# A fused forward and backward kernel: load order and transposes at the start, the gate as row sums, and the last tile in halves

## The chip, the cores and the metric

The kernel runs as one program on one core of one Trainium2 chip. A core has five engines that run at the same time, each through its own instructions in order: TensorE (PE in the profile) multiplies matrices and transposes tiles into PSUM; VectorE (DVE) and ScalarE (ACT) do elementwise work and read PSUM out; GpSimd (POOL) and SyncE (SP) here mostly issue DMAs. Engines wait for each other by semaphores. The metric is the device time of one execution in microseconds (us); lower is better. Three executions of the kernel before took 1215.14, 1215.94 and 1216.46 us, median 1215.94.

## What is computed

A gated mix of two branches, and its gradients for a given `grad_out`:

```python
x = A_x                                               # 1 x 2048 x 1024, bfloat16
g = sigmoid((x * gate_w).sum(-1, keepdims=True))      # one number per row
a = irfft2(rfft2(x) * (w_r + 1j * w_i))               # spectral filter over 2048 x 1024
h = x @ w1 + b1                                       # 1024 -> 3584
b = relu(h) ** 2 @ w2 + b2                            # 3584 -> 1024
out = g * a + (1 - g) * b
# and jax.vjp: the gradients of x, w_r, w_i, w1, b1, w2, b2 and gate_w
```

There are nine outputs: `out` and eight gradients.

## The kernel before

Rows are handled in 16 tiles of 128; the 3584 hidden columns (F) in 28 chunks of 128 (`fc`), 1024 (D) in 8 chunks (`dc`). PE's work is laid out in three main stages: `mlp_in` (hidden products and their gradients), `mlp_grads` (gradients of w1 and w2) and `mlp_out` (the output and the gradient of x). The spectral branch is a side generator (`aside`, L1721), cut into several hundred steps; `spread` (L1607) mixes its steps into the main stages at rates worked out from the number of steps left (`first_rate`, `rate`, `last_rate`; the total is the formula of L1747). The order in which the program emits instructions is the order on each engine, except where a dependency ("paced", `after`, L234) holds one back; a `NoSync` dependency fixes an order on one engine without a wait. DMAs are issued by SP (`ld`), POOL (`st`) or ACT.

**The start.** `mlp_in` first does `fc` 0 to 3 (two w1 pairs `fp` 0 and 1, each of two chunks) for four blocks of 512 rows (`s`), one unit per `next(units)`: for every `s` four hidden units (`forth`, L757) and then four gradient units (`back_`, L763). A hidden unit is 8 products 128x512 `ph` (L725), then on ACT a ReLU `rT` (L726) and a square `h2T` (L727). A gradient unit is 8 products `pd` (L733) and on DVE one scalar_tensor_tensor (L737) with `rT`. The products need x and the gradient transposed: `turn_tile` (L636) makes 8 PE transposes of a row tile into PSUM tile `pt` (two buffers, shared with the gate) and one copy into `xT` (ACT, or DVE for tiles 1 and 3) or `dbT` (DVE). Before a gradient tile is turned it is scaled by 1 - g: `gate` (L649) makes the row sums of x*gate_w for four tiles with 32 PE products one column wide (`pg`, L655) against `gwcol` (the gate row as a column, turned by `vectors`, L643), two sigmoids on ACT (`omg`, `gcol`) and four scalings of `dbn` on DVE (L662).

The loop at L1666 weaves this for each `s`: turning of grad tiles and x tiles, the gate and, behind unit 7, steps of the spectral first stage (11 of them in the start). SP's loads are x0 to x3, w1 pair 0, grad 0 to 3, w1 pair 1, two transposing loads of w2 (L181), x4 to x7, grad 4 to 7, and then the spectral stage's sources (`src`) mixed with the other x and grad tiles. POOL loads the constants `kf`, `flip`, `sel` and `cf` early. x tiles for turning have four buffers (`xsrc`).

**The middle.** In `folded` (L546) of the spectral output stage ACT copies the even parts (`re`, L553) and DVE makes folds `rf` (L558, L559); both are input of PE's products `pki` (L566). The copies are held, by `turn["ACT"]`, behind the newest ordered ACT instruction of the main stage, whatever that is: a copy that frees a PSUM bank, or a scaling in `prepare` (L1254) or `close` (L1264).

**The last stage.** `mlp_out` is made of Strassen-like blocks (`Block`, L1320 on): seven chains of 14 products (`chain`, L1337) on quarter matrices, `p1` to `p7`, into PSUM banks `X` and `V`; ACT copies `X` out (`kept`, L1347: `c1`, `u2`, `u3`), DVE adds a bank and a kept copy into `cu` (L1360). "h" blocks make `out`, "d" blocks the gradient of x. `right` (L1398) makes the differences of right operands `T1` to `T4` on DVE. In the last "h" block (k == NB-1), `right(T1, ...)` (L1503) stands ahead of `put` (L1276) and `prepare` of the next tiles. The last "d" block ends with p5, p7, p4 and p3; between p4 and p3 the gate gradient's row is made (L1590 to L1593). The block's tile 14 is finished by `close_x` (L1309) after p3: DVE adds p3's bank and u2 into cu's right half, adds v over the whole width and SP stores 128x1024.

Of the kernel before, what the change touches and what calls it, by code (L numbers as in the profile page):

```python
# [10 lines left out]
P = 128  # L11
# [129 lines left out]
def kernel(  # L141
# [67 lines left out]
    gwcol = cols("gwcol", [DC], BF16)  # L209
# [31 lines left out]
    turn = {"PE": None, "DVE": None, "ACT": None}  # L241
# [288 lines left out]
    def fft_out():  # L530
# [15 lines left out]
        def folded(n):  # L546
# [5 lines left out]
            for im in range(2):  # L552
# [3 lines left out]
                ), "ACT")  # L556
# [73 lines left out]

    def source(i, view, earlier=None, tag="src"):
        src = f1.tile([P, D], BF16, name=tag, tag=tag, bufs=4)
        after(ld(out=src[:], in_=view[i]), earlier)
        return src

    def turn_tile(dst, i, src, copy):  # L636

        pt = tps.tile([P, DC, P], BF16, name="pt", tag="tr", bufs=2)
        for b in range(DC):
            nc.tensor.transpose(pt[:, b, :], src[:, b * P : (b + 1) * P], identb[:])  # L640
        copy(out=dst[:, :, of_tile(i)], in_=pt[:])

    def vectors(vrow):  # L643
        vps = tps.tile([P, FC + DC], BF16, name="vps", tag="tr", bufs=2)
        nc.tensor.transpose(vps[:], vrow[:], identb[: FC + DC, : FC + DC])
        nc.vector.tensor_copy(out=b1col[:], in_=vps[:, 0:FC])
        nc.vector.tensor_copy(out=gwcol[:], in_=vps[:, FC : FC + DC])

    def gate(i0):  # L649

        c_ = slice(i0, i0 + 4)
        pg = tps.tile([P, 4], FP32, name="pg", tag="tr", bufs=2)
        for i in range(i0, i0 + 4):
            for dc in range(DC):
                mm(  # L655
                    pg[:, i - i0 : i - i0 + 1], lhsT=xT[:, dc, of_tile(i)], rhs=gwcol[:, dc : dc + 1],
                    start=(dc == 0), stop=(dc == DC - 1), skip_group_check=True,
                )
        nc.scalar.activation(omg[:, c_], pg[:], ACT.Sigmoid, scale=-1.0)
        nc.scalar.activation(gcol[:, c_], pg[:], ACT.Sigmoid)  # L660
        for i in range(i0, i0 + 4):
            nc.vector.tensor_scalar(out=dbn[:, i, :], in0=dbn[:, i, :], scalar1=omg[:, i : i + 1], scalar2=None, op0=ALU.mult)  # L662
# [37 lines left out]
    def mlp_in():  # L700
# [20 lines left out]

        def hidden(fc, ss, w1g, h2T, rT):
            ph = bank("ph")
            for dc in range(DC):
                mm(ph[:], lhsT=w1g[:, dc, fc % 2 * P : (fc % 2 + 1) * P], rhs=xT[:, dc, ss], start=(dc == 0), stop=(dc == DC - 1))  # L725
# [3 lines left out]
        def grads(fc, sb, ss, rT, dhT):  # L729
            w_ = w2T[fc // FGC]  # L730
            pd = bank("pd")
            for ec in range(DC):
                mm(  # L733
                    pd[:], lhsT=w_[:, ec, fc % FGC * P : (fc % FGC + 1) * P], rhs=dbT[:, ec, ss],
                    start=(ec == 0), stop=(ec == DC - 1),
                )
# [5 lines left out]
        def load_w2(fg, earlier=None):  # L742

            w2T[fg] = wb.tile([P, DC, FGW], BF16, name="w2T", tag="w2T", bufs=2)
            for h in (0, FGW // 2):
                f0 = fg * FGW + h
                after(turned(w2T[fg][:, :, h : h + FGW // 2], B_w2[f0 : f0 + FGW // 2, :]), earlier)
# [1049 lines left out]
```

## Time and profile before

| | |
|---|---|
| median of 3 executions | 1215.94 us (1215.14 to 1216.46) |
| profiled execution | 1215.59 us |
| its span, first to last instruction | 1213.8 us |
| granted TensorE clock | 0.999 |
| instructions | 20077 |
| PE products `ph` (L725) | 214.6 us busy |
| PE products `pd` (L733) | 210.0 us busy |
| DMA traffic | 234.44 MB, mean 193 GB/s |

The profile is one execution; the busy time of an engine is the time in which an instruction of it ran. The profiled execution lasted 1.8 us longer than its span, and 0.35 us less than the median of the runs. "Idle before" an instruction is the time its engine stood, with what ended it behind an arrow. Matmuls are pipelined: the listed 379 ns of one 128x512 product overlap with the next, and 8 of them take 1.73 us from start to start. 8 transposes of a tile take 0.445 us. The 40 slices of the span show PE and DVE as follows (tenths of a slice, 30 us each):

```profile
PE   9999999999999999999999999999999999999997
...
DVE  3546466586788977887789556665389756966464
```

The last stage begins near 890 us. The copies of turned tiles on DVE take 0.69 us each, on ACT 1.01 us; one scaling of a grad tile 0.42 us.

### The profile page before, as it was taken

How to read it: one execution, taken by the hardware profiler on the slowest of the kernel's cores; microseconds unless marked ns; L12 is line 12 of the kernel's file. 1: busy time of each engine (PE TensorE's matmuls, PEld its weight loads, DVE VectorE, ACT ScalarE, POOL GpSimd, SP SyncE). 2: the span in 40 equal slices, each digit the busy share in tenths (PEclk: the TensorE clock that was granted, in tenths of full speed). 3: DMA queues.
4: the chain of work that ended last, by engine and by line, in shares of the span. 5: the costliest groups of instructions: out<-in, count | busy, mean ns of one | idle time of the engine just before them, and what ended most of it. 6: DMA issues, size and time to landing. Idle time of an engine off the chain costs nothing. (4 is left out here: it accounts for less than half of the span.)

```text
span 1213.8 us, 20077 instructions
## 1 busy us (share of the span) xinstructions
PE 1189.0 (98%) x7229; PEld 653.8 (54%) x7328; DVE 827.5 (68%) x1808; ACT 620.7 (51%) x1128; POOL 361.0 (30%) x587
## 2 busy tenths in 40 slices
PE   9999999999999999999999999999999999999997
PEld 5555555544444444444447889888444444444443
DVE  3546466586788977887789556665389756966464
ACT  4658767736777773444445245554455422332322
POOL 0124424413455542333333434444131000000000
PEclk9999999999999999999999999999999999999999
DMA  9668566486758598998998799956875699965550
GB/s 278 214 173 191 165 170 215 132 168 194 203 178 209 178 242 138 213 221 201 238 207 163 163 250 216 212 170 180 269 217 173 193 212 221 247 198 174 160 148 35
DMA packets 332383, 234.44 MB, mean 193 GB/s; under 512 B 197773, under 2 KB 291115, under 8 KB 332283
## 3 DMA queue, kind: packets, MB, share of 16 engines
q1 hardware_dynamic: 301856, 142.50, 52.2%
q0 software_dynamic: 30224, 90.61, 24.0%
q8 instruction: 57, 0.93, 0.3%
q14 instruction: 44, 0.35, 0.1%
q10 hardware_dynamic: 202, 0.04, 0.0%
HBM read 107.24 MB, written 81.81 MB: 156 GB/s over the span
## 5 line engine op out<-in xcount | busy, mean ns | idle before, releaser
L725 PE MATMUL ph<-xT,w1g 128*128 128x512 bf16 x866 | 214.6, 379 | 3.0 <-DMA w1g<-in_B_w_dram 1.2
L733 PE MATMUL pd<-dbT,w2T 128*128 128x512 bf16 x874 | 210.0, 379 | 1.0
L733 PEld LDWEIGHTS <-w2T 128*128 128x128 bf16 x896 | 87.1, 98 | 101.8
L737 DVE SCALAR_TENSOR_TENSOR dhT<-pd,rT 128x512 bf16<-128x512 f32 x112 | 76.8, 686 | 87.9 <-PE pd L733 76.1
L725 PEld LDWEIGHTS <-w1g 128*128 128x128 bf16 x896 | 85.2, 98 | 93.3 <-DMA w1g<-in_B_w_dram 1.5
L726 ACT ACTIVATE rT<-ph,b1col 128x512 bf16<-128x512 f32 x112 | 77.3, 690 | 67.3 <-PE ph L725 60.4
L987 PEld LDWEIGHTS <-res 128*128 128x128 bf16 (+1 forms) x896 | 86.7, 98 | 12.2 <-issue 2.0
L1339 PEld LDWEIGHTS <-dS 128*128 128x128 f16 x574 | 55.9, 98 | 66.3
L226 POOL DMA_DIRECT2D z_scr<-u x96 | 58.6, 616 | 105.5 <-ACT u L294 51.0
L226 POOL DMA_DIRECT2D r<-y_scr x96 | 58.3, 612 | 104.7 <-issue 44.4
L419 ACT CAST x<-px 64x512 f16<-64x512 f32 x128 | 74.1, 579 | 18.0 <-PE px L416 16.9
L727 ACT ACTIVATE h2T<-rT 128x512 bf16<-128x512 bf16 x112 | 70.6, 630 | 2.1
L987 PEld LDWEIGHTS <-X 128*128 128x128 f16 x672 | 64.7, 98 | 8.0
L1339 PEld LDWEIGHTS <-odd 128*128 128x128 bf16 (+1 forms) x392 | 38.2, 98 | 47.7 <-issue 2.1
L1339 PEld LDWEIGHTS <-even 128*128 128x128 bf16 (+1 forms) x392 | 38.1, 98 | 44.6
L913 PEld LDWEIGHTS <-S 128*128 128x128 f16 x336 | 32.9, 98 | 39.7 <-DVE S L887 0.3
L456 POOL DMA_DIRECT2D y_scr<-pc x64 | 36.3, 567 | 52.7 <-DVE pc L453 43.6
L1360 DVE TENSOR_TENSOR cu<-pV,u 128x512 f16<-128x512 f32 x28 | 19.3, 689 | 44.0 <-PE pV L1339 38.2
L779 POOL DMA_DIRECT2D h2T_scr<-h2T x28 | 20.7, 738 | 95.7 <-ACT h2T L727 95.5
L568 ACT CAST rt<-pki 128x1024 f16<-128x1024 f32 x32 | 32.4, 1013 | 29.2 <-PE pki L566 29.2
L1312 POOL DMA_DIRECT2D out_dram<-gxo x14 | 7.6, 540 | 131.8 <-DVE gxo L1311 131.8
L426 DVE TENSOR_TENSOR tt<-x,w 128x1028 f16<-128x1028 f16 (+1 forms) x32 | 22.2, 693 | 33.8 <-ACT x L420 20.8
(265 smaller groups left out, 2472.8 us busy)
## 6 DMA issues: line engine op xcount, KB each, us to landing
h2T_scr<-h2T POOLq DMA_DIRECT2D x28, 512.0 KB, 4.2
dhT_scr<-dhT POOLq DMA_DIRECT2D x28, 512.0 KB, 5.1
z<-z_scr SPq DMA_DIRECT2D x64, 128.0 KB, 3.3
y_scr<-pc POOLq DMA_DIRECT2D x64, 128.0 KB, 3.8
ax_scr<-yo POOLq DMA_DIRECT2D x32, 256.0 KB, 4.2
w1g<-in_B_w_dram SPq DMA_DIRECT2D x14, 512.0 KB, 4.9
out_dram<-whi POOLq DMA_DIRECT2D x28, 256.0 KB, 4.6
out_dram<-wlo POOLq DMA_DIRECT2D x28, 256.0 KB, 5.3
```

The source lines that it names most:

```text
L226: issue(out=a, in_=b) if stored else issue(out=b, in_=a)
L419: nc.scalar.copy(out=x[lanes[n], c, :, 0:HW], in_=px[lanes[c], n])
L456: st(out=y_scr[:][c, :, :, h].rearrange("r x t l -> (r x) t l"), in_=pc[:, n])
L568: nc.scalar.copy(out=rt[n][:], in_=pk[:])
L725: mm(ph[:], lhsT=w1g[:, dc, fc % 2 * P : (fc % 2 + 1) * P], rhs=xT[:, dc, ss], start=(dc == 0), stop=(dc == DC - 1))
L726: nc.scalar.activation(rT[:], ph[:], ACT.Relu, bias=b1col[:, fc : fc + 1])
L727: nc.scalar.activation(h2T, rT[:], ACT.Square)
L733: mm(pd[:], lhsT=w_[:, ec, fc % FGC * P : (fc % FGC + 1) * P], rhs=dbT[:, ec, ss], start=(ec == 0), stop=(ec == DC - 1),)
L737: return STT(out=dhT, in0=pd[:], scalar=2.0, in1=rT[:], op0=ALU.mult, op1=ALU.mult, accum_out=gb1part[:, fc, sb : sb + 1],)
L913: self.mm = mm(acc[:], lhsT=lhs[:, t, c_], rhs=rhs[:, t, :], start=start and t == 0, stop=t == KH - 1, skip_group_check=True,)
L987: ins = mm(acc[:, j * FH : (j + 1) * FH], lhsT=lhs[:, t, c_], rhs=rhs[:, t, :], start=start and first_ is None, stop=t == KH - 1, skip_gro ...
L1339: pe(mm(acc[:], lhsT=lhs[:, c, :], rhs=rhs[:, c, :], start=start and c == 0, stop=c == KH - 1, skip_group_check=True,))
```

## The change

- **Loads.** All loads of the start stand in one order on SP, tied by `queued`: x0 to x3, w1 pair 1, x4 to x7, grad 0 to 3, the two transposing loads of w2, grad 4 to 7, x8 to x11, grad 8 to 11, x12 to x15, grad 12 to 15, then the spectral sources. w1 pair 0 and the gate row are loaded from ACT's queue ahead of them. The four constants (POOL) come behind the last scaling that was emitted by then (`later["scaled"]`). `xsrc` has eight buffers.
- **Units.** Two blocks at a time: hidden units of s = 0 and 1 (u0 to u7), gradient units of s = 0 and 1 (u8 to u15), then the same for s = 2 and 3 (u16 to u31). Turned tiles have fixed places: x4 ahead of u1, x5 of u2, x6 and x7 of u3, grad 0 to 7 ahead of u4 to u11, x8 to x15 ahead of u12 to u19, grad 8 to 15 ahead of u20 to u27; each is tied behind the last product before it and the next product behind it. Of the copies into `xT` only tile 1's is on DVE. The spectral side starts later, with 6 steps in the start.
- **Gate.** The products `pg` are gone. `everywhere` makes the gate row on all partitions (two products with one row, a copy on ACT); `weigh` makes a tile's row sums with one tensor_tensor_reduce on DVE. It stands ahead of the tile's transposes in the program.
- **Order of copies.** The `re` copies are held behind the newest PSUM copy of the main stage (`turn["copy"]`), not behind any ordered ACT instruction.
- **T1.** In the last "h" block `right(T1, ...)` comes behind `put` and `prepare`.
- **The end.** In the last "d" block u3's chain and copy (`u3_kept`) and `prepare_x` come ahead of p5. For tile 14 the left half is finished and stored before p4, v + u2 is added ahead for the right half, and p3 runs as two chains of 256 columns, each followed by one add and one store of 256 columns.

The order that follows on DVE in the start: copy of x1, b1col, row sums 0 to 4, scaling of grad 0 to 3, row sums 5 to 7, copy of grad 0, scaling of grad 4 to 7, row sum 8, copy of grad 1, row sum 9, grad 2, row sums 10 and 11, grad 3, scaling of 8 and 9, grad 4, and so on. On ACT: copies of x0, the gate row, x2, x3, then for each hidden unit `rT` and `h2T`, with the copies of x4 to x7 and the sigmoids between them.

```diff
@@ -206,7 +206,7 @@
...
     gcol, omg, gpg, bGo, dsc = (cols(n, [NT]) for n in ("gcol", "omg", "gpg", "bGo", "dsc"))
-    gwcol = cols("gwcol", [DC], BF16)
+    gsum = cols("gsum", [NT])
@@ -238,7 +238,7 @@
             tc.add_manual_dep(ins.ins, earlier.ins.name, info, reason="paced")
-    turn = {"PE": None, "DVE": None, "ACT": None}
+    turn = {"PE": None, "DVE": None, "ACT": None, "copy": None}
@@ -553,7 +553,7 @@
...
                     in_=rv[:, im, :, 0::2, :].rearrange("p h g i -> p g h i"),
-                ), "ACT")
+                ), "copy")
@@ -628,38 +628,54 @@
...
     xs = {}
+    def queued(ins):
+        after(ins, later.get("row"), mybir.DependencyClass.NoSync)
+        later["row"] = ins
+
     def source(i, view, earlier=None, tag="src"):
-        src = f1.tile([P, D], BF16, name=tag, tag=tag, bufs=4)
-        after(ld(out=src[:], in_=view[i]), earlier)
+        src = f1.tile([P, D], BF16, name=tag, tag=tag, bufs=8 if tag == "xsrc" else 4)
+        loaded = ld(out=src[:], in_=view[i])
+        if earlier is None:
+            queued(loaded)
+        after(loaded, earlier)
         return src
-    def turn_tile(dst, i, src, copy):
+    def turn_tile(dst, i, src, copy, tie=None):
...
         for b in range(DC):
-            nc.tensor.transpose(pt[:, b, :], src[:, b * P : (b + 1) * P], identb[:])
+            later["turned"] = nc.tensor.transpose(pt[:, b, :], src[:, b * P : (b + 1) * P], identb[:])
+            after(later["turned"], tie, mybir.DependencyClass.NoSync)
...
     def vectors(vrow):
-        vps = tps.tile([P, FC + DC], BF16, name="vps", tag="tr", bufs=2)
-        nc.tensor.transpose(vps[:], vrow[:], identb[: FC + DC, : FC + DC])
-        nc.vector.tensor_copy(out=b1col[:], in_=vps[:, 0:FC])
-        nc.vector.tensor_copy(out=gwcol[:], in_=vps[:, FC : FC + DC])
+        vps = tps.tile([P, FC], BF16, name="vps", tag="tr", bufs=2)
+        nc.tensor.transpose(vps[:], vrow[:], identb[:FC, :FC])
+        later["b1"] = nc.vector.tensor_copy(out=b1col[:], in_=vps[:])
+
+    def everywhere(grow, ones):
+        pb = fps.tile([P, D], FP32, name="pgw", tag="ps2", bufs=2)
+        for h in range(2):
+            later["gate_row"] = mm(pb[:, h * H : (h + 1) * H], lhsT=ones, rhs=grow[:, h * H : (h + 1) * H], start=True, stop=True)
+        gwb = f1.tile([P, D], BF16, name="gwb", tag="gwb")
+        nc.scalar.copy(out=gwb[:], in_=pb[:])
+        return gwb
+
+    def weigh(i, src):
+        unused = f1.tile([P, 2, H], FDT, name="uv", tag="uv", bufs=2)
+        weighed = nc.vector.tensor_tensor_reduce(
+            out=unused[:].rearrange("p a b -> p (a b)"), in0=src[:], in1=gwb[:], scale=1.0, scalar=0.0,
+            op0=ALU.mult, op1=ALU.add, accum_out=gsum[:, i : i + 1],
+        )
+        after(weighed, later.get("b1"), mybir.DependencyClass.NoSync)
...
         c_ = slice(i0, i0 + 4)
-        pg = tps.tile([P, 4], FP32, name="pg", tag="tr", bufs=2)
+        nc.scalar.activation(omg[:, c_], gsum[:, c_], ACT.Sigmoid, scale=-1.0)
+        nc.scalar.activation(gcol[:, c_], gsum[:, c_], ACT.Sigmoid)
         for i in range(i0, i0 + 4):
-            for dc in range(DC):
-                mm(
-                    pg[:, i - i0 : i - i0 + 1], lhsT=xT[:, dc, of_tile(i)], rhs=gwcol[:, dc : dc + 1],
-                    start=(dc == 0), stop=(dc == DC - 1), skip_group_check=True,
-                )
-        nc.scalar.activation(omg[:, c_], pg[:], ACT.Sigmoid, scale=-1.0)
-        nc.scalar.activation(gcol[:, c_], pg[:], ACT.Sigmoid)
-        for i in range(i0, i0 + 4):
-            nc.vector.tensor_scalar(out=dbn[:, i, :], in0=dbn[:, i, :], scalar1=omg[:, i : i + 1], scalar2=None, op0=ALU.mult)
+            later["scaled"] = nc.vector.tensor_scalar(out=dbn[:, i, :], in0=dbn[:, i, :], scalar1=omg[:, i : i + 1], scalar2=None, op0=ALU.mult)
@@ -719,10 +735,15 @@
         later["more_banks"] = more_banks
+        def opened(ins, fc):
+            if fc < 4:
+                after(ins, later["turned"], mybir.DependencyClass.NoSync)
+                later["product"] = ins
+
...
             for dc in range(DC):
-                mm(ph[:], lhsT=w1g[:, dc, fc % 2 * P : (fc % 2 + 1) * P], rhs=xT[:, dc, ss], start=(dc == 0), stop=(dc == DC - 1))
+                opened(mm(ph[:], lhsT=w1g[:, dc, fc % 2 * P : (fc % 2 + 1) * P], rhs=xT[:, dc, ss], start=(dc == 0), stop=(dc == DC - 1)), fc)
@@ -730,10 +751,10 @@
...
             for ec in range(DC):
-                mm(
+                opened(mm(
...
                     start=(ec == 0), stop=(ec == DC - 1),
-                )
+                ), fc)
@@ -744,18 +765,27 @@
...
                 f0 = fg * FGW + h
-                after(turned(w2T[fg][:, :, h : h + FGW // 2], B_w2[f0 : f0 + FGW // 2, :]), earlier)
+                loaded = turned(w2T[fg][:, :, h : h + FGW // 2], B_w2[f0 : f0 + FGW // 2, :])
+                after(loaded, earlier)
+                if fg == 0:
+                    queued(loaded)
...
         rows_ = lambda s: slice(s * SW, (s + 1) * SW)
-        def load_w1(fp):
+        def load_w1(fp, issue=ld):
             w1[fp] = wb.tile([P, DC, PW], BF16, name="w1g", tag="w1g", bufs=2)
-            ld(out=w1[fp][:], in_=w1v[:, :, fp * PW : (fp + 1) * PW])
+            loaded = issue(out=w1[fp][:], in_=w1v[:, :, fp * PW : (fp + 1) * PW])
+            if fp == 1:
+                queued(loaded)
         def forth(fp, s, c):
-            rT = rTs[fp, s, c] = wb.tile([P, SW], BF16, name="rT", tag="rT", bufs=6)
+            if fp < 2 and s % 2 and fp:
+                rT = f1.tile([P, SW], BF16, name="rTe", tag="rTe", bufs=2)
+            else:
+                rT = wb.tile([P, SW], BF16, name="rT", tag="rT", bufs=6)
+            rTs[fp, s, c] = rT
@@ -780,19 +810,22 @@
             st(out=dhT_scr[2 * fp : 2 * fp + 2, :, cols2].rearrange("c p s -> p c s"), in_=dhT[:])
-        load_w1(0)
+        load_w1(0, nc.scalar.dma_start)
...
         load_w1(1)
+        yield
...
         yield
-        for s in range(4):
+        for pair in range(2):
             for what in (forth, back_):
-                for fp in range(2):
-                    for c in range(2):
-                        what(fp, s, c)
-                        yield
-            if s == 2:
-                load_w1(2)
+                for s in (2 * pair, 2 * pair + 1):
+                    for fp in range(2):
+                        for c in range(2):
+                            what(fp, s, c)
+                            yield
+                if pair and what is forth:
+                    load_w1(2)
+            if not pair:
@@ -969,7 +1002,7 @@
...
                 t_ = sb.tile([P, H], FP32, name=name, tag=name, bufs=bufs)
-                turn["ACT"] = nc.scalar.copy(out=t_[:], in_=self.X[:])
+                turn["ACT"] = turn["copy"] = nc.scalar.copy(out=t_[:], in_=self.X[:])
@@ -1347,6 +1380,7 @@
...
                 act(nc.scalar.copy(out=t_, in_=self.X[:]))
+                turn["copy"] = turn["ACT"]
@@ -1382,9 +1416,12 @@
...
             def p7(self):
+                self.u3_kept()
+                self.add(1, R, self.V, self.u3)
+
+            def u3_kept(self):
...
                 self.u3 = self.kept("u3", 1)
-                self.add(1, R, self.V, self.u3)
@@ -1431,6 +1468,7 @@
...
             act(nc.scalar.copy(out=fresh(t)[:, (L, R)[hf]], in_=acc[:]))
+            turn["copy"] = turn["ACT"]
@@ -1499,11 +1537,11 @@
...
                 pass
-            if last:
-                right(T1, qs[1], qs[0])
...
             prepare(2 * k + 1), prepare(2 * k)
+            if last:
+                right(T1, qs[1], qs[0])
@@ -1574,24 +1612,41 @@
...
                 a.p3()
+            if last:
+                prepare_x(2 * k), prepare_x(2 * k + 1)
+                b.u3_kept()
...
             b.sums(4)
-            prepare_x(2 * k), prepare_x(2 * k + 1)
+            if not last:
+                prepare_x(2 * k), prepare_x(2 * k + 1)
...
                 dve(nc.vector.reduce_sum(out=part, in_=rows_, axis=mybir.AxisListType.X))
-            b.p7()
+            if last:
+                b.add(1, R, b.V, b.u3)
+            else:
+                b.p7()
...
         a.done = lambda t: close_x(t, ld)
+        t_ = 2 * (NB - 1)
+        c_, v_, o_ = cu.pop(t_), v.pop(t_), row("gxo", BF16, tag="ot")
+        dve(V(out=o_[:, L], in0=c_[:, L], in1=v_[:, L], op=ALU.add))
+        ld(out=o1_perm[t_][:, L], in_=o_[:, L])
+        dve(V(out=c_[:, R], in0=v_[:, R], in1=a.u2, op=ALU.add))
...
         st(out=out_8.rearrange("(b c) -> b c", c=32), in_=row_)
-        a.p3()
+        for j in range(2):
+            c2 = slice(j * H // 2, (j + 1) * H // 2)
+            d2 = slice(H + j * H // 2, H + (j + 1) * H // 2)
+            a.chain(a.V[:, c2], a.S[4], a.B["22"][:, :, c2], False)
+            dve(V(out=o_[:, d2], in0=a.V[:, c2], in1=c_[:, d2], op=ALU.add))
+            ld(out=o1_perm[t_][:, d2], in_=o_[:, d2])
@@ -1623,13 +1678,15 @@
...
         for i in range(4 * k, 4 * (k + 1)):
-            ld(out=dbn[:, i, :], in_=go_perm[i])
+            queued(ld(out=dbn[:, i, :], in_=go_perm[i]))
     def turn_x(i):
-        turn_tile(xT, i, rows.pop(i), nc.vector.tensor_copy if i in (1, 3) else nc.scalar.copy)
+        src = rows.pop(i)
+        weigh(i, src)
+        turn_tile(xT, i, src, nc.vector.tensor_copy if i == 1 else nc.scalar.copy, later["gate_row"] if i == 2 else later.get("product"))
     def turn_grad(i):
-        turn_tile(dbT, i, dbn[:, i, :], nc.vector.tensor_copy)
+        turn_tile(dbT, i, dbn[:, i, :], nc.vector.tensor_copy, later["product"])
@@ -1645,58 +1702,49 @@
...
     units = mlp_in()
+    vrow = f1.tile([FC, P], BF16, name="vrow", tag="vrow")
+    nc.scalar.dma_start(out=vrow[:], in_=B_b1.rearrange("(fc p) -> fc p", p=P))
+    grow = f1.tile([1, D], BF16, name="grow", tag="grow")
+    nc.scalar.dma_start(out=grow[:], in_=gate_w.rearrange("(o d) -> o d", o=1))
+    next(units)
+    ones = f1.tile([1, P], BF16, name="ones", tag="ones")
+    nc.vector.memset(ones[:], 1.0)
     rows_of_x(0)
-    vrow = f1.tile([FC + DC, P], BF16, name="vrow", tag="vrow")
-    nc.scalar.dma_start(out=vrow[0:FC, :], in_=B_b1.rearrange("(fc p) -> fc p", p=P))
-    nc.scalar.dma_start(out=vrow[FC : FC + DC, :], in_=gate_w.rearrange("(fc p) -> fc p", p=P))
     next(units)
+    rows_of_x(1)
     rows_of_grad(0)
...
+    gwb = everywhere(grow[:], ones[:])
...
         turn_x(i)
...
+        warm((0, 2, 2, 0)[i])
+        if i == 1:
+            vectors(vrow)
+    gate(0)
     next(units)
...
+    rows_of_grad(1)
+    rows_of_x(2)
+    rows_of_grad(2)
+    rows_of_x(3)
+    rows_of_grad(3)
+    for t_, n in ((kf, "kf"), (flip, "flip"), (sel, "sel"), (cf, "cf")):
+        after(st(out=t_[:], in_=cten[n].ap()), later["scaled"])
     stage = None
...
+    before = {1: [4], 2: [5], 3: [6, 7], **{u: [u - 4] for u in range(12, 20)}}
+    grads_before = {**{u: [u - 4] for u in range(4, 12)}, **{u: [u - 12] for u in range(20, 28)}}
+    for u in range(32):
+        for i in before.get(u, ()):
+            turn_x(i)
+        for i in grads_before.get(u, ()):
+            turn_grad(i)
         next(units)
...
+        if u in (3, 15, 19):
+            gate({3: 4, 15: 8, 19: 12}[u])
+        if u == 17:
...
             stage = first_stage_of_x()
...
+        if u > 19 and u % 2:
+            next(stage)
...
```

## The prediction

> **What bounds the kernel.** I read the page's busy times first, then its chain, then PE's list of waits, then the timelines of the first 35 us and the last 14 us, then the busy times by window.
>
> ```profile
> PE 1189.0 (98%) x7229; PEld 653.8 (54%) x7328; DVE 827.5 (68%) x1808; ACT 620.7 (51%) x1128; POOL 361.0 (30%) x587
> ...
> PE 33%; DVE 5%; issue 2%; DMA 2%; SPq 1%; ACT 1%; POOL 0%; DVEq 0%; ACTq 0%
> ```
>
> PE is busy for 1189.0 of 1213.8 us. Only three things can make this kernel faster: less PE work, fewer PE waits, or a shorter time after PE's last instruction. The list of PE's waits says how little there is to remove (columns: total us, times, longest):
>
> ```profile
> PE pki L566 <- DVE rf L558: 2.4, 7, 0.8
> PE pX L1339 <- ACT u L1349: 1.5, 2, 0.9
> PE pki L566 <- ACT re L553: 1.5, 1, 1.5
> PE pV L987 <- DVE wlo L924: 1.5, 1, 1.5
> PE ph L725 <- DMA w1g<-in_B_w_dram: 1.2, 1, 1.2
> ```
>
> **Gate on VectorE.** The gate's matmuls are on PE alone in the start, and they go.
>
> ```profile
> L655 PE MATMUL pg<-gwcol,xT x128: 163/163/167, 12.5 to 67.9; 128*128 128x1 bf16 x128
> ```
>
> Those 163 ns overlap; in the timeline, the product behind each group of 32 starts 0.80 to 0.82 us after the group does. Four groups: -3.2 us of PE. In their place DVE gets 16 row sums (`weigh`). The nearest row is another row sum over 128x1024 with an accumulator (L1269), 1.23 us and 0.08 for its read: 1.3 us each, 21 us of DVE. The gate row's broadcast costs PE two one-row products, and ACT a copy of 1.0 us (its 128x1024 casts), before the first product. In the first 35 us DVE was mostly idle, so most of this lies beside PE. Not all, because DVE runs in order.
>
> **First product.** The new issue of the first w1 tile is on ACT's queue, at the start.
>
> ```profile
> 10.71 1.90 PE L725 MATMUL ph<-xT,w1g 128*128 128x512 bf16 x7 [1.25 <-DMA w1g<-in_B_w_dram]
> ```
>
> Its data (issued at 2.60) landed at 10.67. Issuing it first could save the 1.25 us, yet the same bytes (x0 to x3, w1 pairs 0 and 1) stand ahead of the product, and ACT must now copy x0, the gate row, x2 and x3 (3.9 us behind x2's landing at 6.77). I take 10.4: -0.3, between -1.2 (the whole wait) and +0.3.
> [...]
>
> **Order of loads and units.** Before, the four grad products of a block follow its four hidden ones; after, 8 hidden units (u0 to u7) come first, then 8 grad units (u8 to u15). x4 to x7 are turned before u1 to u3, grad 0 to 7 one at a time before u4 to u11.
> PE's side: 10.4 + 8 units x 1.73 us + 4 turned x tiles and 5 grad tiles x 0.445 = 28.25. ACT has, from 12.2 on, four pairs of ReLU and square (0.69 + 0.63), four copies of x (0.96) and two sigmoids, some 8.2 us that end with x7's copy at about 20.4, where PE could start u4 at 19.4: +1.0, so u8 could start at 29.2. The same amount of work in before (10.71 + 17.85 of units and turned tiles + two gates, 1.6) ends at 30.2. So PE alone would be 1.0 ahead at u8.
> DVE's side is worse. Its new order there is: copy of grad 0, the scaling of grad 4 to 7, row sum 8, grad 1, row sum 9, grad 2, row sums 10 and 11, grad 3. u8 needs the copies of grad 0 to 3, and they now stand behind four row sums of x tiles that u8 doesn't need. From T8, the landing of x8: 4 x 1.3 + 3 x 0.65 (the copies, 0.69 long) = 7.15 us, plainly more than x9 to x11's pace of 0.67 us per tile. u8 starts at T8 + 7.15 or at 29.2, whichever is later.
>
> ```profile
> 8.16 9.63 SPq L181 DMA_TRANSPOSE w2T<-in_B_w_dram  x2
> ...
> 17.91 1.93 SPq L633 DMA_DIRECT2D xsrc<-in_A_x_dram  x4
> 19.89 1.87 SPq L1626 DMA_DIRECT2D dbn<-in_grad_out_dram  x4
> ```
>
> These are SP's issues in before. The fifth load behind the two transposed loads (dbn 4) landed at 25.10. In the new order the fifth is x8, and eight 256 KB tiles instead of four precede the transposed loads; by this analogy T8 is 25.1 to 26.5. By bytes it is earlier: 6.56 MB (9 x tiles and 8 grad tiles of 0.262, four weight loads of 0.524) land up to x8, and before moved 3.04 MB in 12 us and 5.26 MB in the next 18, which is 6.56 MB at 24.0. Before also had a dip to 75-240 GB/s at 4.5 to 7 us, with the constants' loads on POOL (kf, cf) in it; those loads now wait for the last scaling, which nothing on PE needs before u20. I take 24.2, near the byte end because that dip goes: u8 at 31.35, 1.2 behind before. Behind it, two later gates are gone (-1.6), the change of banks with STT still running costs 0.35, and ACT's sigmoids and copies ahead of u20 0.55, both estimates from the ACT and DVE rows above. **Start in all: +0.5**, where the gate's 3.2 is nearly given back; from -1.7 (u8 at 29.2) to +2.8 (T8 = 26.5).
>
> **Middle.** The `re` copies are ordered only behind the copies that free PSUM: the one wait of 1.5 on them may go. Against it, 5 steps of spectral work leave the start and run later, with the spectral tail ending 84 products later in the last stage, where DVE has little room:
>
> ```profile
> 640.00:660.00 20.00, 19.95 (x153) 14.97 (x153) 19.91 (x33) 9.71 (x18) 8.11 (x14) 1.00 0.81 158
> 660.00:680.00 20.00, 18.48 (x164) 15.82 (x163) 19.07 (x35) 9.61 (x18) 6.75 (x10) 1.00 0.58 133
> 680.00:700.00 20.00, 20.00 (x186) 17.92 (x184) 6.57 (x8) 4.12 (x8) 10.85 (x18) 1.00 1.06 209
> ```
>
> (Window, length, then PE, PEld, DVE, ACT, POOL.) DVE is full from 640 to 680, with PE's wait for `wlo` of 1.5 us in it, and has 13 us free in the next 20. I put the lateness at +0.7 (half of that wait again): -0.8, from -1.5 to the rival's +8 below. T1's subtraction moves behind the tiles' `prepare` and `put`:
>
> ```profile
> 1028.43 3.88 DVE L1399 TENSOR_TENSOR wT<-w1q,w1q 128x7168 f16<-128x7168 bf16 x1
> 1032.23 0.68 DVE L1278 TENSOR_TENSOR ot<-even,na 128x1024 bf16<-128x1024 f16 x1
> ```
>
> Behind its 3.88 us stood ot, v, na and then ACT's `u` at 1033.91, for which PE waited 0.9: -0.9. T1 itself is wanted only by p5 of the next block, several products of 3.1 us later; should that cover go, +0.9 at most comes back.
>
> **Tail.**
>
> ```profile
> 1201.56 3.18 PE L1339 MATMUL pX<-wT,odd 128*128 128x512 f16 x14 [0.67 <-ACT u L1349]
> ...
> 1204.85 3.20 PE L1339 MATMUL pV<-w2L,dS 128*128 128x512 bf16 x13
> 1208.08 0.69 DVE L1360 TENSOR_TENSOR cu<-pV,u 128x512 f16<-128x512 f32 x1 [1.91 <-PE pV L1339]
> 1208.81 0.69 DVE L1311 TENSOR_TENSOR gxo<-cu,g 128x1024 bf16<-128x1024 f16 x1
> ```
>
> With u3's chain ahead of p5, p4 needn't wait 0.67; p3 is then held only by the add that frees its bank, which ends at 1204.14 behind gacc's transpose and reduction: about 1204.4 instead of 1204.85, -0.45 (0 to -0.67). At the end two DVE steps (0.69 + 0.69 + 0.04 between) become one of 256 columns from PSUM; 16-bit rows of half width show 0.29 against 0.42, so I take 0.42 (0.35 to 0.69): -1.0. The halved store (64 KB): the 256 KB store took 2.02 us from issue to landing and a 2 KB one 1.88, so at most 0.14, I take 0.1. **Tail: -1.55**, from -0.7 to -1.9.
> [...]
>
> **Sum.** +0.5 - 0.8 - 0.9 - 1.55 = -2.75 from the profiled 1215.59 (span 1213.8 and 1.8 around it): 1212.84. The median of the runs is 0.35 above that execution: **1213.2**. Its own range, with T8 below 25: 1209.7 to 1215. 0.2% is 2.4 us, about what a measurement of this kernel tells from no change: faster is below 1213.5, slower above 1218.4.
>
> **Rivals.**
> *Handed back (0.20):* the loads are late as in before's analogy, T8 = 25.3 to 26.5. u8 starts at 32.5 to 33.7, the start costs +1.6 to +2.8, and the sum is 1214.3 to 1215.5. For it: SP's 9.63 us of issuing transposed loads lie in front of grad 4. Against: the bytes.
> *Slower (0.24):* the five late steps, 1.25 turns of the middle spectral stage at 6.4 us of DVE each, 8 us, fall in the full stretch 640 to 680 and PE waits them out: 1213.2 + 8 = 1221. It becomes slower once PE waits for 5.2 us of the 8. For it: 39 of 40 us are busy there. Against: 13.4 us of DVE are free from 680 on, and the rate of the side work is computed anew from what is left.
> *Full gain (0.17):* x8 lands by 22.1, no row sum is late, u8 starts at 29.2; the start brings -1.7: 1211.0, and 1209.7 if the middle brings its 1.5 and more of the 1.25 us of first wait goes.
> *It stays at the end (in the main case's range):* the time from the last store to the span's end, 1209.87 to 1213.8, is unchanged by the halves, so the tail can't bring more than 1.9.
>
> **Chances.** Main case 0.39 (0.32 of it faster), handed back 0.20 (0.02 faster), slower 0.24, full gain 0.17: faster 0.51, same 0.25, slower 0.24. Range 1208.5 to 1219.5: below it, little of the full gain, above it, half of the slower case.
>
> **What would show it.** No pg rows; first ph at about 10.4; u4 waiting about 1 us for ACT's xT; the first pd at 31.4, with PE waiting on DVE's dbT behind row sums whose own wait is on the xsrc loads; no `re` wait and no `u` wait at 1033; last store issued near 1208.0 in a trace otherwise like before, earlier by what start and middle bring. Wrong, if the first pd is before 30 or after 33, if PE's waits on DVE between 600 and 700 grow by more than 2 us, or if the row sum costs much other than 1.3 us.

## The result and the profile after

The changed kernel took 1214.37 us (median of four executions, 1212.87 to 1215.68) against 1215.75 before: a ratio of 0.9988, with a 95% interval of 0.9971 to 1.0005, so no change that can be told. Twelve more executions in a later job gave 1214.31 and 0.9979 (0.9961 to 0.9997), just clear of 1. The profiled execution is the slowest of the four: 1215.68 us, span 1213.9, against 1215.59 and 1213.8 before. It shows well where the gate's 3.2 us went. PE's waits after the change (columns: total us, times, longest):

```profile
PE pt L647 <- DVE dbT L649: 2.4, 1, 2.4
PE pV L1020 <- DVE wlo L957: 2.0, 1, 2.0
PE pd L754 <- DVE dbT L649: 1.9, 1, 1.9
PE ph L746 <- ACT xT L649: 1.6, 1, 1.6
...
PE pki L566 <- ACT re L553: 0.8, 2, 0.6
...
PE pX L1372 <- DVE dS L1368: 0.5, 1, 0.5
PE pV L1372 <- DVE gxo L1648: 0.5, 1, 0.5
```

The waits on `dbT` are new, 4.4 us in all. PE's timeline shows where they stand:

```profile
9.99 1.89 PE L746 MATMUL ph<-xT,w1g 128*128 128x512 bf16 x8 [1.57 <-ACT xT L649]
...
28.08 0.61 PE L647 MATMUL pt<-identb,dbn 128*128 128x128 bf16 x8 [2.42 <-DVE dbT L649]
...
32.81 3.29 PE L754 MATMUL pd<-dbT,w2T 128*128 128x512 bf16 x8 [1.95 <-DVE dbT L649]
35.89 0.93 PE L647 MATMUL pt<-identb,dbn 128*128 128x128 bf16 x8
36.66 1.89 PE L754 MATMUL pd<-dbT,w2T 128*128 128x512 bf16 x8
```

The first wait is for one of `pt`'s two buffers: grad 3 can't be turned until grad 1's copy is out. The second is for grad 3's copy. VectorE's timeline in the same stretch:

```profile
23.45 1.08 DVE L678 TENSOR_SCALAR dbn<-dbn,omg 128x1024 bf16<-128x1024 bf16 x2 [2.35 <-DMA dbn<-in_grad_out_dram]
...
26.19 1.22 DVE L666 CUSTOM_DVE_ANT_0 uv<-xsrc,gwb 128x1024 f16<-128x1024 bf16 x1
...
27.34 0.68 DVE L649 COPY dbT<-pt 128x1024 bf16<-128x1024 bf16 x1
27.95 1.21 DVE L666 CUSTOM_DVE_ANT_0 uv<-xsrc,gwb 128x1024 f16<-128x1024 bf16 x1
...
29.09 0.68 DVE L649 COPY dbT<-pt 128x1024 bf16<-128x1024 bf16 x1
...
31.98 0.69 DVE L649 COPY dbT<-pt 128x1024 bf16<-128x1024 bf16 x1
```

VectorE first waits for grad 4's load (23.45) and scales grad 4 to 7 as they land, up to 26.1, when x8 has just landed too (26.06). Then each row sum stands ahead of the copy of a grad tile; grad 1 had been in PSUM since 21.8 us. Four row sums and three copies take 6.4 us (starts 1.15 and 0.60 apart), so the first grad product starts at 32.81 instead of some 28. Its 8 products then take 3.08 us (32.81 to 35.89) instead of 1.73. The windows say why; the column after the busy times is the granted clock:

```profile
32.00:33.00 1.00, 0.19 (x1) 0.13 (x2) 1.00 (x5) 0.88 (x4) 0.00 (x0) 1.00 1.05 395
33.00:34.00 1.00, 1.00 (x4) 0.40 (x3) 1.00 (x4) 0.63 (x1) 0.08 (x1) 0.57 1.04 401
34.00:35.00 1.00, 1.00 (x3) 0.30 (x2) 1.00 (x4) 0.00 (x0) 0.64 (x1) 0.50 1.06 404
```

PE ran at half clock for some 3.4 us: 1.7 us more, with PE counted as busy.

The account of the two profiled executions, in us: first product -0.72 (10.71 to 9.99); gates -3.2; waits from the first product to 60 us +3.9 (4.37 against 0.49); half clock +1.7; later waits up to p4's end -2.5 (7.04 against 9.54); from p4's end to the span's end +0.2 (9.29 against 9.08). That sums to -0.6; the spans differ by +0.1, and 0.7 stays unassigned.

### The profile page after: what moved, and what is told of

The parts are those of the page before. It is cut to its first block, busy times and chain, and to the rows that moved or that the text cites. A ratio compares the mean times of both kernels' runs of the same rounds, so it can differ in the third digit from the quotient of the medians.

```text
span 1213.9 us, 19997 instructions
## 1 busy us (share of the span) xinstructions
PE 1192.4 (98%) x7213; PEld 651.6 (54%) x7213; DVE 844.2 (70%) x1841; ACT 624.5 (51%) x1130; POOL 364.4 (30%) x587
## 5 line engine op out<-in xcount | busy, mean ns | idle before, releaser
L746 PE MATMUL ph<-xT,w1g 128*128 128x512 bf16 x896 | 218.8, 379 | 1.6 <-ACT xT L649 1.6
L754 PE MATMUL pd<-dbT,w2T 128*128 128x512 bf16 x896 | 213.6, 381 | 1.9 <-DVE dbT L649 1.9
L758 DVE SCALAR_TENSOR_TENSOR dhT<-pd,rT 128x512 bf16<-128x512 f32 x108 | 74.2, 687 | 77.3 <-PE pd L754 62.8
L747 ACT ACTIVATE rT<-ph,b1col 128x512 bf16<-128x512 f32 x108 | 74.5, 690 | 47.2 <-PE ph L746 46.9
L748 ACT ACTIVATE h2T<-rT 128x512 bf16<-128x512 bf16 x108 | 68.0, 630 | 2.2
L394 POOL COPY w<-wn 128x512 bf16<-128x512 bf16 x32 | 23.1, 721 | 84.3 <-DVE tt L427 66.3
L1372 PE MATMUL pX<-wT,dS 128*128 128x512 f16 x196 | 44.8, 379 | 0.5 <-DVE dS L1368 0.5
```

Of the source, the lines that this page charges most:

```text
L746: opened(mm(ph[:], lhsT=w1g[:, dc, fc % 2 * P : (fc % 2 + 1) * P], rhs=xT[:, dc, ss], start=(dc == 0), stop=(dc == DC - 1)), fc)
L747: nc.scalar.activation(rT[:], ph[:], ACT.Relu, bias=b1col[:, fc : fc + 1])
L748: nc.scalar.activation(h2T, rT[:], ACT.Square)
L754: opened(mm(pd[:], lhsT=w_[:, ec, fc % FGC * P : (fc % FGC + 1) * P], rhs=dbT[:, ec, ss], start=(ec == 0), stop=(ec == DC - 1),), fc)
L758: return STT(out=dhT, in0=pd[:], scalar=2.0, in1=rT[:], op0=ALU.mult, op1=ALU.mult, accum_out=gb1part[:, fc, sb : sb + 1],)
L1372: pe(mm(acc[:], lhsT=lhs[:, c, :], rhs=rhs[:, c, :], start=start and c == 0, stop=c == KH - 1, skip_group_check=True,))
```

## The experiments

In this section "the first grad product" is the first `pd`, and "p4's end" the end of the last chain into bank X; all numbers are of the profiled execution unless called a median. A ratio is to the kernel before in the same job, with its 95% interval.

**The changed kernel again.**

> The changed kernel once more, beside the same runs of the kernel before as the three edits that follow. Its profile has two PE waits at the copies of turned grad tiles (2.42 us ahead of grad 3's transposes, 1.95 ahead of the first grad product) and a granted clock of 0.50 to 0.57 from 33 to 36 us. If that is a fixed part of this kernel, waits of 4.4 us in all and a low clock for some 3.5 us show again and the time is within 2 us of 1214.4. If the low clock came by chance in one execution, it is absent here and the time is about 1.7 us lower (1212.7).

Median 1214.31. The waits and the half clock are there again, but at another place: half clock from 27.95 to 31.36, beginning inside a first wait of 2.65 us (25.73 to 28.38), so the eighth hidden unit was slow (2.80 us) and the second wait shrank to 0.50; the two waits come to 3.15 us, not 4.4. The first grad product started at 33.10. The stall is part of the kernel, and half clock came in both profiles of it.

**Row sums behind the copies.** The edit is one tie without a wait, on VectorE's own order:

```diff
         after(weighed, later.get("b1"), mybir.DependencyClass.NoSync)
+        if i >= 8:
+            after(weighed, later["dbT", min(i - 4, 7)], mybir.DependencyClass.NoSync)
```

> Only the order on VectorE is changed: the row sums of x8 to x15 are tied behind the copies of turned grad tiles 4 to 7. Theory (row sums of tiles that nobody needs yet stand in VectorE's order ahead of copies that TensorE needs): grad 1's copy comes right behind the scaling of grad 7 (26.1 us), PE's wait ahead of grad 3 is about 1.1 us instead of 2.42, the wait of 1.95 ahead of the first grad product goes, that product starts at 29.4 instead of 32.8, and if the low clock came from those two waits it goes too: 5 us less than the changed kernel (1.7 of them the clock). Rival (the loads of grad 4 to 7 and x8 set the pace, whatever the order): the first grad product stays at 32 or later and the time within 1 us of the changed kernel's.

PE's timeline of this kernel:

```profile
26.91 0.61 PE L647 MATMUL pt<-identb,dbn 128*128 128x128 bf16 x8 [0.80 <-DVE dbT L649]
...
29.52 1.89 PE L756 MATMUL pd<-dbT,w2T 128*128 128x512 bf16 x8
```

Median 1212.11, ratio 0.9963 (0.9945 to 0.9981). PE waits 0.80 ahead of grad 3, the first grad product starts at 29.52, the clock stays at 1.00 in the start. From first product to p4's end it is 2.9 us less than the changed kernel, although half clock came later in this profile, from 668.8 to 672.2, behind PE's wait for `wlo` (1.7 us). The median is 2.2 us lower, not the 5 expected. The order was the cause of all but 0.8 us of the waits; what is left stands behind the scalings, which wait for loads.

**Scalings behind the copies too.**

```diff
-        if u in (3, 15, 19):
-            gate({3: 4, 15: 8, 19: 12}[u])
+        if u in (6, 15, 19):
+            gate({6: 4, 15: 8, 19: 12}[u])
...
+            if i0 == 4:
+                after(later["scaled"], later["dbT", 2], mybir.DependencyClass.NoSync)
```

> As the kernel with the row sums moved, and the scaling of grad 4 to 7, which waits for loads that land at 23.4 to 25.4 us, is moved behind the copies of grad 0 to 2. Theory: no PE wait over 0.3 us between 12 and 40 us, first grad product at 28.3 us, no low clock, 6.2 us less than the changed kernel (4.4 us of waits, 1.7 of clock), so about 1208.2 and 0.994 of the kernel before. Rival (the middle of the kernel gives it back, because side work then meets a busier VectorE): first grad product at 28.3 us, but the time less than 3 us below the changed kernel.

PE's timeline of this kernel has no wait from 11.8 us on in the start; four of its lines:

```profile
25.43 0.61 PE L647 MATMUL pt<-identb,dbn 128*128 128x128 bf16 x8
25.88 1.89 PE L750 MATMUL ph<-xT,w1g 128*128 128x512 bf16 x8
27.61 0.61 PE L647 MATMUL pt<-identb,dbn 128*128 128x128 bf16 x8
28.05 1.89 PE L758 MATMUL pd<-dbT,w2T 128*128 128x512 bf16 x8
```

Median 1210.57, ratio 0.9929 (0.9894 to 0.9965); 3.7 below the changed kernel's median, not 6.2. The profile shows one reason: as in the kernel above, half clock came later, at another wait that these kernels have (1.99 us for `wlo` near 665):

```profile
660.00:667.00 7.00, 4.56 (x39) 3.73 (x39) 6.29 (x10) 5.55 (x10) 1.57 (x3) 1.00 0.42 104
667.00:671.00 4.00, 4.00 (x24) 2.94 (x22) 3.80 (x8) 0.00 (x0) 3.91 (x8) 0.57 0.68 197
```

The same wait of 1.98 us in both profiles of the changed kernel was followed by full clock. A kernel further below, equal to this one up to the last tile, was profiled without any half clock there: from first product to p4's end it took 1187.9 us, against 1194.6 in the changed kernel, which is the 6.2 expected and 0.5 more.

**Dummy products in the waits.** Before grad 3's transposes stand 9 products of zeros, before the first grad product 7; ties keep VectorE's order up to there:

```diff
+        if u == 7:
+            fill(9)
         for i in grads_before.get(u, ()):
             turn_grad(i)
+        if u == 8:
+            fill(7)
```

> The changed kernel with 9 dummy products of zeros on PE in the first wait and 7 in the second (0.216 us each, 1.94 of 2.42 us and 1.51 of 1.95), and ties that keep VectorE's order up to the first grad product. Theory (the clock is lowered because PE stood still): the first grad product starts at 32.8 as before, the granted clock stays at 1.00 from 30 to 40 us, the first 8 grad products take 1.73 us instead of 3.08, and the time is 1.7 us below the changed kernel. Rival (the clock drops for another cause, or through the load of the first grad products): the clock is 0.8 from 30 to 40 us as before and the time is the same within 0.7 us.

PE's two waits shrank to 0.48 and 0.43 us, the first 8 grad products take 1.73 us, and the windows are at full clock:

```profile
30.00:35.00 5.00, 4.57 (x34) 2.37 (x32) 5.00 (x11) 1.50 (x4) 0.73 (x1) 1.00 1.05 392
35.00:40.00 5.00, 4.50 (x36) 2.48 (x34) 5.00 (x10) 0.00 (x0) 0.00 (x0) 1.00 1.04 393
```

The first grad product starts at 32.84, as in the changed kernel. So the half clock went with the two waits (2.42 and 1.95 us in the changed kernel, 0.48 and 0.43 here, one profile each), not with the load of the products. The time did not fall: median 1216.14, ratio 0.999 (0.9967 to 1.0012). The edit moved a row sum on VectorE ahead of later work, and two new waits of 0.50 and 0.62 us followed (at 37.4 and 42.5). That is 1.1 of the 1.7 us; why the median is above the changed kernel's isn't settled.

**The gate alone.** The kernel before with row sums instead of `pg`, each behind the grad copies before it:

```diff
-        pg = tps.tile([P, 4], FP32, name="pg", tag="tr", bufs=2)
...
+        src = rows[i]
+        turn_tile(xT, i, src, nc.vector.tensor_copy if i in (1, 3) else nc.scalar.copy)
+        if i > 3:
+            after(weigh(i, rows.pop(i)), later["dbT"], mybir.DependencyClass.NoSync)
```

> The kernel before with one part of the change: the gate as row sums on VectorE (each behind the copies of the grad tiles turned before it), with the old order of loads and units and the old end. Theory (the gate's 3.2 us on PE are a real gain wherever PE does not wait for the row sums): PE waits about 0.8 us for the first scaled grad tile (four row sums of 1.15 us from 9.65 on, sigmoid, scaling, so 15.0 instead of 14.2), nothing else new over 0.5 us, and the time is 2 to 2.5 us below the kernel before (0.998). Rival (the old order of units needs the gate earlier, so the row sums are late at every block): PE waits of more than 2 us in all between 14 and 70 us on scaled grad tiles or on dhT, and the time is within 1 us of the kernel before.

Median 1214.91, ratio 1.0005 (0.9987 to 1.0024). Neither came: the row sums were in time, but PE, with less to do, caught up with the old order of loads. Its list of waits:

```profile
PE ph L733 <- DMA w1g<-in_B_w_dram: 1.8, 2, 0.9
...
PE pt L640 <- DMA xsrc<-in_A_x_dram: 1.4, 1, 1.4
```

2.3 us of these stand behind the first product (w1 pair 1 at 14.0, x4 at 20.3). In the old order of loads most of the gate's gain becomes a wait for data. That the new order of loads and units makes room for it fits the kernels above, whose start has no such wait; no run has the new order with the old gate.

**T1's place**, in the kernel with row sums and scalings moved:

```diff
+            if last:
+                right(T1, qs[1], qs[0])
             if a is not None:
                 put(2 * k - 2)
             prepare(2 * k + 1), prepare(2 * k)
-            if last:
-                right(T1, qs[1], qs[0])
```

> The kernel with row sums and scalings moved, with T1's subtraction put back ahead of put and prepare in the last h block. Theory: PE waits about 0.9 us for ACT's u again, as at 1033 us in the kernel before, and p3 starts 0.9 us later. Rival (the wait came from the older state of the side work): no PE wait over 0.3 us between 1010 and 1040 us.

```profile
PE pX L1376 <- ACT u L1386: 0.9, 1, 0.9
```

The wait is back (0.87 at 1029), where without this edit there is none. This step of the change brings 0.9 us: from first product to p4's end this kernel takes 0.8 us more than the one with `out_8` from SP below, which is the same up to there but for T1 (one execution each, both without half clock).

**The order of the `re` copies**, again in that kernel (`turn["ACT"]` in place of `turn["copy"]`):

```diff
-                ), "copy")
+                ), "ACT")
```

> The kernel with row sums and scalings moved, with the even copies of the spectral output stage ordered behind any ordered ACT instruction again, as before the change. Theory (that order made PE's wait of 1.5 us for re in the kernel before): PE's waits for re grow from 0.8 us in two to about 1.5 or more, and p3 ends about 0.7 us later behind the first product. Rival (re waits on loads or on ACT's own queue anyway): the waits for re stay within 0.3 us of 0.8.

```profile
PE pki L566 <- ACT re L553: 1.5, 4, 0.6
...
PE pki L566 <- DVE rf L559: 1.1, 4, 0.4
PE pki L566 <- DVE rf L558: 0.9, 4, 0.4
```

`re`'s waits grow by 0.7, but `rf`'s (L558) fall from 1.4 to 0.9: where two inputs are late, taking one away leaves the other. From first product to p4's end it is 0.3 us more than in the kernel with `out_8` from SP below, which is the same up to there; each is one execution.

**Side work earlier.**

```diff
-        return 0.0 if left_[0] < 6 else 1.6 if "mid" in later else 1.75
+        return 0.0 if left_[0] < 6 else 1.65 if "mid" in later else 1.80
```

> The kernel with row sums and scalings moved, with the rates of the spectral side work in the first stage raised from 1.75 and 1.6 to 1.80 and 1.65 steps per pair of units, so that about 5 steps more are done by its end, as many as the start has lost. Theory (the late side work costs PE waits where VectorE is full, 640 to 680 us): PE's waits for wlo and whi (2.0 and 0.6 us) fall to the 1.5 us of the kernel before or below, and the time falls by 0.5 to 1.1 us. Rival (the lateness costs nothing): those waits stay at 2.4 to 2.7 us and the time is within 0.5 us.

```profile
PE pX L1024 <- DVE G L1072: 2.0, 1, 2.0
...
PE pv L447 <- DVE y L440: 0.9, 1, 0.9
...
PE pV L1024 <- DVE wlo L961: 0.5, 2, 0.3
```

The waits for `wlo` and `whi` fell from 2.6 to 0.9 us in all, and others came (`G` 2.0 at 812, `y` 0.95 at 410, `pb` 0.7). Median 1210.09, ratio 0.9955 (0.9927 to 0.9983), not to be told from the kernel it is compared with. The lateness makes those waits, but the work waits elsewhere when it is moved.

**The last tile as a whole.** One chain, one add, one store of 128 KB:

```diff
+        a.chain(a.V[:], a.S[4], a.B["22"], False)
+        dve(V(out=o_[:, R], in0=a.V[:], in1=c_[:, R], op=ALU.add))
+        ld(out=o1_perm[t_][:, R], in_=o_[:, R])
-        for j in range(2):
...
```

> The kernel with row sums and scalings moved, with p3 of the last tile as one chain of 512 columns, one add and one store of 128 KB instead of two halves. Theory (the second half waits for the first half's add, 0.5 us, and two short chains take longer, so halving loses on PE what it wins on the add): p3 lasts 3.2 us instead of 3.9, the add 0.69 instead of 0.42, the store leaves 0.4 us earlier, and the span after p3's start shrinks from 9.15 to about 8.7 us. Rival (the halves pay, by the shorter last store): the span after p3's start is the same or longer, 9.15 us or more.

From p4's end the store leaves after 4.1 us instead of 4.5, as the theory has it, yet the span ends after 9.30 instead of 9.28: no gain from the earlier store, and none from the halves. So something else ends the span. The sequencers' last instructions in the traces show it (DRAIN is one that stands at the end of each engine's program): SP's drain ends 1.8 us before the span does in the kernel before and 2.9 us in the changed one, while POOL's drain begins with its last store and lasts 6.60 and 6.52 us, with 0.8 us of closing steps behind it. In the ten profiles up to this one the span ends 7.26 to 7.35 us after POOL's issue of the 2 KB store of `out_8`. POOL's timeline of the changed kernel:

```profile
1197.30 0.54 POOL L1345 DMA_DIRECT2D out_dram<-gxo  x1 [5.61 <-DVE gxo L1344]
1206.64 0.54 POOL L1643 DMA_DIRECT2D out_dram<-w2R  x1 [8.79 <-DVE w2R L1642]
```

1206.64 + 7.27 = 1213.91, its span. That store leaves 2.0 us after p4's end here and 1.7 before, since two new DVE adds stand ahead of `row_`; with 7.27 us behind it for 7.35 before, this is the +0.2 of the account.

**`out_8` from SP**, in the kernel before, and in the kernel with row sums and scalings moved:

```diff
-        st(out=out_8.rearrange("(b c) -> b c", c=32), in_=row_)
+        ld(out=out_8.rearrange("(b c) -> b c", c=32), in_=row_)
```

> The kernel before with one edit: the last store of the gate's gradient (out_8, 2 KB) is issued by SP instead of POOL. In all ten profiles so far the span ends 7.26 to 7.35 us after POOL issues that store, and SP has finished 1.8 to 3.1 us before the span's end. Theory (POOL's drain behind its last store sets the end, not the output store): POOL's last store is then one of some 10 us earlier, the end follows SP's drain (1212.0 us in the profile before) by about 0.8 us, and the span is about 1.0 us shorter (1212.8 for an otherwise equal execution); from p4's end to the span's end 8.1 us instead of 9.06. Rival (the end is a fixed time behind the last data store, whoever issues what): 9.0 us from p4's end to the span's end, time unchanged.

> The kernel with row sums and scalings moved, and out_8's store on SP. Theory: the end follows SP's drain, which came 6.4 us after p4's end, so 7.2 us from p4's end to the span's end instead of 9.27, and 2.1 us less time than the kernel with row sums and scalings moved (some 1208.3 against 1210.5). Rival: 9.2 us from p4's end to the end, time unchanged.

From p4's end to the span's end: 7.99 us instead of 9.08 in the kernel before, 7.09 instead of 9.28 in the other, and in both the span ends 0.75 to 0.77 behind SP's drain. POOL's drain is what ended the span. In time, the kernel before with this edit gave 1215.07 against 1215.95, ratio 1.0005 (0.9978 to 1.0032): unclear, and its profiled execution was disturbed at the start (x3 landed at 10.87 instead of 8.14, half clock from about 13 us). The other gave a median of 1207.57, ratio 0.9924 (0.9903 to 0.9945), 3.0 us below the kernel with row sums and scalings moved, which ran in another job (2.1 expected).

**Whole, with `out_8` from SP.**

> As the one with out_8's store on SP, and p3 of the last tile as one chain, one add and one store. With POOL's drain out of the way the halves can be judged. Theory (halving costs PE 0.7 us and saves 0.27 us of add and some landing time): SP's drain comes 6.2 us after p4's end instead of 6.4, and the span ends 0.2 us earlier than with halves, 7.0 us after p4's end. Rival (the halves pay once nothing else holds the end): the whole chain ends later than the halves, 7.4 us or more after p4's end.

6.90 us from p4's end, SP's drain after 6.14 instead of 6.34. The last lines of PE and DVE, first with halves, then whole:

```profile
1200.39 1.69 PE L1376 MATMUL pV<-w2L,dS 128*128 128x256 bf16 x14 [0.52 <-DVE gxo L1652]
...
1202.12 0.42 DVE L1652 TENSOR_TENSOR gxo<-pV,cu 128x256 bf16<-128x256 f32 x1 [1.78 <-PE pV L1376]
```

```profile
1199.74 3.18 PE L1376 MATMUL pV<-w2L,dS 128*128 128x512 bf16 x14
...
1202.96 0.69 DVE L1649 TENSOR_TENSOR gxo<-pV,cu 128x512 bf16<-128x512 f32 x1 [1.65 <-PE pV L1376]
```

The second half waits 0.52 for the first half's add on the same bank. Whole is 0.2 us better at the end, in one profile each; the medians don't tell the two apart. This is the fastest kernel of the study: median 1206.78 (1206.46 to 1208.25), ratio 0.9915 (0.9894 to 0.9937).

## The prediction, step by step

- *The outcome* was not the likeliest one: 1214.37 is 1.2 above the forecast of 1213.2, within the main case's range, but as a change it can hardly be told. It is the rival "handed back", which gave 1214.3 to 1215.5: x8's landing and the first grad product fell inside its ranges (25.3 to 26.5, and 32.5 to 33.7). That its time fits too is partly luck: its price for the start, +1.6 to +2.8, is met only with the half clock, which it did not have, and the tail, taken at -1.55 in it, brought -0.5 (p4's wait -0.67, the end +0.2). The profiled pair differs by +0.1 us, where the forecast's terms came to -2.75.
- *The step that failed in size* is T8, "I take 24.2, near the byte end". x8 landed at 26.06, inside the analogy's 25.1 to 26.5: the transposing loads began at 11.77 and ended their issue at 19.19, and grad 4 (23.35) to x8 followed behind them at 0.68 us each. The place behind the transposing loads told the landing, the count of bytes did not.
- *VectorE's order* was the right mechanism; its 7.15 us measured 6.4 (starts 1.15 and 0.60 apart, not durations), so the first grad product came at 32.81 for a forecast of 31.35; with 7.15, a landing at 26.06 would have put it at 33.2. Not foreseen: the first half of the stall comes one unit earlier, through `pt`'s two buffers.
- *The half clock* (+1.7) was in no step. The start was forecast to cost 0.5 and cost 1.7 by the account above; without the half clock it would have cost nothing. The two estimates in it, 0.35 for the change of banks and 0.55 for ACT ahead of u20, show in no wait: from the first product to 60 us PE has only the two on `dbT`.
- *First product*: -0.72 (forecast -0.3). w1 pair 0 landed at 9.70 instead of 10.67, and x0 to x3 no later than before (x3 at 7.65 for 8.14); but the constants' loads had left this stretch too, and no run separates the two. *x7's copy*: no wait of 1.0; it ended at 19.38 and PE was ready at 19.39. The forecast's 8.2 us on ACT is the sum for three pairs of ReLU and square, not for the four it names; three stood ahead of that copy.
- *Gate*: no `pg` left; the kernel before with the gate alone shows that its 3.2 us mostly aren't PE's to keep in the old order of loads.
- *Middle*: -0.8 forecast. The later waits without T1 and p4 fell by 1.0, of which the `re` order is 0.3, not 1.5. *T1*: -0.9, shown. The rival of 8 us did not come; PE's waits near 665 grew by 1.1.
- *Tail*: -1.55 forecast. p4's wait of 0.67 went (it is among the account's later waits). Behind p4, p3 lasted 3.89 us for 3.20; the 1.0 us of shorter DVE work came, and the last store, of 64 KB, took 1.53 us from issue to landing where 256 KB had taken 2.02: 0.5 less, not 0.1. All of that lay beside POOL's drain and did not reach the end. I had taken the last store for the end of the span without looking at what each engine does behind its last transfer.

## What to carry to other kernels

Work moved to an idle engine still takes a place in its order: a row sum whose data comes late holds everything behind it, and one tie that puts it behind the urgent copies took away 3.6 of the 4.4 us of waits that it had made. Look at what each engine does after its last transfer before shortening the last one; here a 2 KB store on GpSimd's queue set the end, 7.27 us behind its issue in the changed kernel. There a wait of 1.95 us on TensorE was followed by 3.41 us at half clock, another 1.7 us, while the 1.98 us for `wlo` was not.

## What the runs showed of the hardware

Up to PE's last product, half clock came in stretches of 3.41 us, at PE waits of 1.84 us (with two shorter ones just before it), 1.99, 1.95 (with one of 2.42 just before it), 2.65 and 2.98 us; the same 1.99 us wait for `wlo` was followed by it in four kernels' profiles (1.7 us of PE each) and by full clock in five others. One thing that differs is where the wait lies. The clock's record keeps one value for 1204.905 us in the kernel before, and for 27.307, 3.413 and 1174.185 us in the changed one: 353, 8, 1 and 344 times 3.4133, to 0.002 us. Counted in steps of that length from a change of the clock in the same profile, the wait lay whole inside one step in the changed kernel (the 1.95, from 30.86 to 32.81, in the step from 29.72 to 33.13), in the kernel with row sums and scalings moved (the 1.99, from 664.54 to 666.53, in 663.97 to 667.38) and in the one with the last tile whole (the wait for `wlo`, some 666.9 to 668.9, in 666.5 to 669.9), and the next step ran at half clock. In the changed kernel the 2.42 and the 1.98 for `wlo` were split over two steps (0.64 and 1.78, 0.30 and 1.68), and the clock stayed full; so it did behind a wait of 1.52 us whole inside one step in the kernel before, and behind one wait for `wlo` whole inside a step, 0.03 us behind its start, in another profile. The wait of 2.65 us had 2.2 in one step, and the next ran at half clock. The wait of 2.98 us, 1.57 in one and 1.41 in the next, was followed by half clock and does not fit so simply.

POOL's drain behind its last DMA, the 2 KB of `out_8`, lasted 6.60 us in the kernel before and 6.52 us in the changed one; both are variants of this one program.
